# The last product of a fused attention and two-MLP kernel, from a plain tiled product to Strassen's seven products in [column, token] layout

## The chip, the cores and the metric

The kernel runs on one core of one Trainium2 chip. A core has five engines with queues of their own: TensorE (PE, matrix products; its weight loads are listed as PEld), VectorE (DVE), ScalarE (ACT), GpSimd (POOL) and SyncE (SP, which here only issues transfers). Sixteen DMA engines carry the transfers that SP and ACT issue. The metric is the device time of one execution in microseconds.

## The reference

Attention within chunks of 64 tokens (8 batches, 8 heads, 576 tokens, 64 wide), then two MLPs on 4608 tokens of 512 columns, in float32:

```python
x = attention(q, k, v)                       # 4608 x 512
h = np.maximum(x @ moe_w_in, 0.0)            # 512 -> 2048
y = h * h @ moe_w_out                        # 2048 -> 512
g = y @ moe2_w_gate                          # 512 -> 1536
val = y @ moe2_w_val                         # 512 -> 1536
out = (g * (1 / (1 + np.exp(-g))) * val) @ moe2_w_out   # 1536 -> 512
```

The last line's product, 4608 x 1536 by 1536 x 512, is what the change is about.

## The kernel before

Every float32 operand of a large product is split into a high part, rounded to the type that TensorE takes (`fp32r`), and a low part, the difference: `split` (line 419) lets ScalarE cast the high part (line 154) and VectorE subtract for the low one (line 157). `three` (line 400) then issues three matmuls, high by high, low by high and high by low, into one PSUM bank. Weights come as 64-bit words and are decoded to float32 by ScalarE, VectorE and GpSimd (`decode1` to `decode3`) before they are split.

Tokens are worked in 9 blocks of 512; `sets` pairs them as (0), (1, 2), (3, 4), (5, 6), (7, 8). The input product of the first MLP and the gate and value product of the second (class `Products`, with `Pair` for two blocks and `Single` for one) use Strassen's scheme in Winograd's form: seven products of half-sized blocks in place of eight, with sums of weights (seven combinations per pair of weight rows, `prep_pair`) and sums of tokens (`Operands`). There the weights stand in the array and 512 tokens move. A partial sum `x` in PSUM is added to by products 1, 6, 7 and 4 one after another, and ScalarE keeps copies of it on the way (`kept`, line 469; r1, u2, u3). Of the weight combinations of the gate and value product two keys of twelve stay in SBUF, the other ten are loaded again for each set (`load_combo`, line 228), three keys ahead.

The results of the gate and value product, h, are stored in DRAM (`valued`, line 591) and read back by the last product, class `Down` (line 736). It goes block by block; for each of 12 weight rows f and each of 4 groups of 128 tokens it issues `three` with the token slice of h standing and the weight row of 512 columns moving (`use2`, line 919). Four accumulators of 128 tokens by 512 columns fill four banks. At the block's end ScalarE and VectorE copy them, alternately, and SP stores each with runs of 2 KB (`evict2`, line 923). The 12 split weight rows are prepared during the last set of the gate and value product (`prep_plain`, line 165) and stay in SBUF.

The order of instructions is a planner's, which simulates the engines, except inside `ordered(...)` blocks, where the named engines keep the order of the program. TensorE's order is the program's in the gate and value product (line 909); in the last product it is the planner's. `Work` (line 233) holds prepared steps that are called beside the products: `beside2` (line 888) takes one step at every second of the 48 quarters of the last set until eight quarters before its end, then starts the last product's loads. A tile of a pool takes a buffer when one comes free; its first writer waits for that. The pool `big` has 31 buffers of 4 KB per partition, `wp` five of 14 KB, `small` six of 2 KB; PSUM has six single banks and one double one.

Of the kernel before, what the change touches and what calls it, by code (L numbers as in the profile page):

```python
# [20 lines left out]
P = 128  # L21
# [7 lines left out]
def attention_mlp_mlp_kernel(  # L29
# [135 lines left out]
    def prep_plain(name, f, raws):  # L165

        raw = raws.take(1)
        yield
        m = one("m").rearrange("p (t c) -> p t c", t=1)
        decode1(raw, m)  # L170
        decode2(raw, m)
        decode3(raw, m)
        w = duo("w", F32R)
        parts_of(m[:, 0, :], w[:, 0, :], w[:, 1, :])
        plain[name, f] = w
        yield
# [51 lines left out]
    def load_combo(key):  # L228
        w = new_combo()
        nc.sync.dma_start(out=flat(w), in_=wdram[key])  # L230
        combos[key] = w

    class Work:

# [289 lines left out]
    def dram(name, n):  # L524
        return [[dp.tile([P, 2, BLOCK], F32, name=f"{name}{b}_{i}") for i in range(n)] for b in range(nb)]

    ydram = dram("y", kt // 2)
    g1dram, g2dram = dram("g", nf1 // 2), dram("h", nf2 // 2)

    def squared(bs, fp):  # L530

# [44 lines left out]
    def valued(bs, fp):  # L576

        g = gates.pop((bs, fp))
        left = [2] * len(bs)

        def take(i, j, ps, r):
            o = g[j][:, i, :]
            if r is None:
                nc.vector.tensor_tensor(out=o, in0=ps, in1=o, op=ALU.mult)
            else:
                c = one("c")
                add(c, ps, r)
                nc.vector.tensor_tensor(out=o, in0=c, in1=o, op=ALU.mult)
            left[j] -= 1
            if left[j] == 0:  # L590
                nc.sync.dma_start(out=g2dram[bs[j]][fp], in_=g[j])

        return take


    work = Work()
    n1, n2 = nf1 // 2, nf2 // 2

    keys1 = [("i", fp) for fp in range(n1)]
    keys2 = [(name, fp) for fp in range(n2) for name in "gv"]  # L600
# [172 lines left out]
                if i == n - 1:  # L773
                    evict(b, acc)

    down1, down2 = Down(g1dram, n1), Down(g2dram, n2)

# [108 lines left out]
    def beside2(n, m):  # L888
        def at_quarter(i):
            t = 4 * m + i - 4 * len(keys2)  # L890
            if n + 1 < len(sets):
                if t == -24:
                    for b in sets[n + 1]:
                        yraw[b] = load_y(b)
                if t == -8:
                    y_sums(n + 1)
                if t in OPS:
                    up2.ops[n + 1].make(*OPS[t])
            else:
                if t % 2 == 0 and t < -8:  # L900
                    work.step(1)
                if t == -8:
                    down2.begin()
                if t == -4:
                    down2.split(0)

        return at_quarter

    with ordered(ET.PE):
        for n in range(len(sets)):  # L910
            if n + 1 == len(sets):
                raws = Raws(w_out2, 2)
                for f in range(nf2):
                    work.add(prep_plain("p", f, raws))
            for m in range(len(keys2)):
                up2.run(n, m, beside2(n, m))
        up2.finish()

    def use2(acc, t, w, g, first, last):
        cols = slice(t * P, (t + 1) * P)  # L920
        three(acc, (g[0][:, cols], g[1][:, cols]), (w[:, 0, :], w[:, 1, :]), first, last)

    def evict2(b, acc):
        for t in range(4):
            o = one("o")
            (nc.vector.tensor_copy if t % 2 else nc.scalar.copy)(out=o, in_=acc[t])
            nc.sync.dma_start(out=out[b * BLOCK + t * P:b * BLOCK + (t + 1) * P, :], in_=o)

    down2.run("p", use2, evict2, lambda b, i: work.step(1))


# [48 lines left out]
```

## Time and profile before

| | before |
|---|---|
| median of 3 runs | 1717.14 us (1717.08 to 1720.78) |
| profiled execution | 1717.07 us, span 1715.3 us |
| mean granted TensorE clock | 0.984 |
| busy TensorE, VectorE, ScalarE, GpSimd | 96%, 51%, 45%, 8% |
| DMA | 385.05 MB, mean 224 GB/s |

The span runs from the first to the last instruction; the rest of the time lies around it. In the rows further below, times are in microseconds and a mean of one instruction in ns; L157 is line 157 of the kernel. In the windows the engines stand in the order PE, PEld, DVE, ACT, POOL, each with its busy time and its count of instructions. A matmul's record is longer than the step from one to the next, because matmuls are pipelined. "idle before" is the time for which an engine stood idle ahead of an instruction, and the names behind it are what ended that.

### The profile page before, as it was taken

To read this page: it belongs to the slowest core of one execution; us is meant where nothing else is said; L and a number is where in the kernel's file an instruction comes from. 1 tells how busy PE (TensorE), PEld (TensorE's weight loads), DVE (VectorE), ACT (ScalarE), POOL (GpSimd) and SP (SyncE) were. 2 spreads that over 40 slices of the span, in tenths; PEclk is the share of its full clock that TensorE was granted. 3 is DMA by queue.
4 is the path that set the end of the run, shared out by engine and by line. 5 is a ranking of instruction groups with operands and counts; after the bars stand their busy time and mean duration, and the time that the engine had idled before them with its cause. 6 is when DMAs were issued, how large, how long until landed. Compare 5 with 4: busy or idle time off the path is not lost.

```text
span 1715.3 us, 23439 instructions
## 1 busy us (share of the span) xinstructions
PE 1641.8 (96%) x9552; PEld 1353.1 (79%) x9552; DVE 880.9 (51%) x1094; ACT 770.4 (45%) x1090; POOL 130.0 (8%) x94
## 2 busy tenths in 40 slices
PE   3878999999999999999999999999999999999998
PEld 3756777778888888888888788787887888888887
DVE  7875464645477656652313547446556666222220
ACT  5775676768775444442212434334335444222210
POOL 3220000010122111100000000000000110000000
PEclk9889999999999999999999999999999999999999
DMA  8557687878875767773329566566668855334431
GB/s 334 208 221 241 240 291 251 290 267 292 321 257 215 289 250 289 270 288 123 111 85 378 195 256 236 207 250 221 220 229 309 308 178 208 117 119 146 123 99 49
DMA packets 88380, 385.05 MB, mean 224 GB/s; under 512 B 9552, under 2 KB 9552, under 8 KB 77392
## 3 DMA queue, kind: packets, MB, share of 16 engines
q1 hardware_dynamic: 77904, 345.80, 57.2%
q10 hardware_dynamic: 10368, 37.75, 5.8%
q8 instruction: 75, 1.23, 0.3%
q14 instruction: 33, 0.27, 0.0%
HBM read 267.91 MB, written 112.46 MB: 222 GB/s over the span
## 4 chain that ended last, share of the span: by engine, by line
PE 87%; DVE 5%; DMA 4%; ACT 2%; issue 1%; SPq 1%; POOL 0%; ACTq 0%; DVEq 0%; POOLq 0%
PE acc L404 10%; PE acc L405 10%; PE acc L403 10%; PE px L403 8%; PE px L405 8%; PE px L404 8%; PE pz L405 4%; PE py L403 4%; PE pz L404 4%; PE pz L403 4%; PE py L405 4%; PE py L404 4%; PE accs L404 4%; PE accs L403 4%; PE accs L405 4%; DMA k<-in_k_dram 4%
## 5 line engine op out<-in xcount | busy, mean ns | idle before, releaser
L157 DVE TENSOR_TENSOR lo<-graw,hi 128x1024 fp32r<-128x1024 f32 x126 | 157.0, 1249 | 222.6 <-PE acc L404 153.9
L403 PE MATMUL px<-hi,W 128*128 128x512 f32 x640 | 251.9, 394 | 5.7 <-ACT hi L154 5.5
L405 PE MATMUL px<-lo,W 128*128 128x512 f32 x640 | 250.2, 391 | 3.1 <-DVE lo L157 3.1
L404 PE MATMUL px<-hi,W 128*128 128x512 f32 x640 | 249.8, 390 | 0.0
L154 ACT CAST hi<-graw 128x1024 fp32r<-128x1024 f32 x126 | 132.2, 1050 | 231.9 <-DVE lo L157 192.6
L139 POOL TENSOR_TENSOR m<-m,raw 128x512 int32<-128x512 int32 x68 | 93.1, 1383 | 1042.0 <-DVE m L135 899.3
L471 ACT COPY u<-px 128x512 f32<-128x512 f32 x160 | 92.5, 578 | 154.6 <-PE px L405 154.6
L403 PE MATMUL acc<-hi,w 128*128 128x512 f32 x416 | 161.8, 389 | 0.0
L404 PE MATMUL acc<-hi,w 128*128 128x512 f32 x416 | 161.8, 389 | 0.0
L405 PE MATMUL acc<-lo,w 128*128 128x512 f32 x416 | 161.5, 389 | 0.0
L403 PEld LDWEIGHTS px<-hi,W 128*128 128x128 f32 x640 | 120.9, 189 | 32.7 <-ACT hi L154 6.3
L405 PEld LDWEIGHTS px<-lo,W 128*128 128x128 f32 x640 | 120.5, 188 | 29.5 <-DVE lo L157 4.2
L404 PEld LDWEIGHTS px<-hi,W 128*128 128x128 f32 x640 | 120.9, 189 | 24.9
L572 DVE TENSOR_TENSOR g<-g,sig 128x1024 f32<-128x1024 f32 x54 | 69.5, 1287 | 132.5 <-ACT sig L571 132.5
L457 DVE TENSOR_TENSOR g<-pz,u 128x512 f32<-128x512 f32 x112 | 76.9, 687 | 113.6 <-PE pz L405 73.6
L403 PE MATMUL pz<-hi,W 128*128 128x512 f32 x320 | 125.8, 393 | 5.4 <-ACT hi L154 5.4
L405 PE MATMUL pz<-lo,W 128*128 128x512 f32 x320 | 126.2, 394 | 3.3 <-DVE lo L157 3.3
L403 PE MATMUL py<-hi,W 128*128 128x512 f32 x320 | 128.1, 400 | 0.0
L405 PE MATMUL py<-lo,W 128*128 128x512 f32 x320 | 126.2, 394 | 0.3 <-DVE lo L157 0.3
L404 PE MATMUL py<-hi,W 128*128 128x512 f32 x320 | 126.3, 395 | 0.0
L404 PE MATMUL pz<-hi,W 128*128 128x512 f32 x320 | 125.5, 392 | 0.0
L404 PE MATMUL acc<-w,lo 128*128 128x512 f32 x312 | 121.4, 389 | 0.0
(103 smaller groups left out, 2878.5 us busy)
## 6 DMA issues: line engine op xcount, KB each, us to landing
W<-wv SPq DMA_DIRECT2D x30, 1792.0 KB, 8.4
g<-g ACTq DMA_DIRECT2D x72, 512.0 KB, 4.8
graw<-g SPq DMA_DIRECT2D x72, 512.0 KB, 4.4
W<-wi SPq DMA_DIRECT2D x20, 1792.0 KB, 9.2
W<-wg SPq DMA_DIRECT2D x20, 1792.0 KB, 7.9
h<-g SPq DMA_DIRECT2D x54, 512.0 KB, 7.6
graw<-h SPq DMA_DIRECT2D x54, 512.0 KB, 3.7
raw<-in_w_out_dram SPq DMA_DIRECT2D x28, 512.0 KB, 8.0
```

The lines of the kernel that those rows point to most:

```text
L139: nc.gpsimd.tensor_tensor(out=mi[:, t, :], in0=mi[:, t, :], in1=word(raw, 0, I32), op=ALU.add)
L154: nc.scalar.copy(out=hi, in_=src)
L157: nc.vector.tensor_tensor(out=lo, in0=src, in1=hi, op=ALU.subtract)
L403: nc.tensor.matmul(out=ps, lhsT=lh, rhs=rh, start=first, stop=False, skip_group_check=on)
L404: nc.tensor.matmul(out=ps, lhsT=ll, rhs=rh, start=False, stop=False, skip_group_check=on)
L405: nc.tensor.matmul(out=ps, lhsT=lh, rhs=rl, start=False, stop=last, skip_group_check=on)
L457: nc.vector.tensor_tensor(out=o, in0=ps, in1=r, op=ALU.add)
L471: nc.scalar.copy(out=r, in_=self.x)
L572: nc.vector.tensor_tensor(out=g[j], in0=g[j], in1=s, op=ALU.mult)
```

## The change

The last product now uses the seven products as well, with columns standing and tokens moving. For pairs of blocks, the contraction's 1536 rows are cut into even and odd halves of h by the index c, the 512 output columns into two halves. `prep_last` decodes a pair of weight rows, forms the seven combinations of 128x256, splits them and stores them in DRAM (`vdram`), one tensor for each product; it replaces `prep_plain` in the last set, with more steps taken per quarter. `load_last` brings all six pairs of one product's weights into one `wp` buffer, or, for products 7 and 3, into three `big` buffers. Class `Last` runs the products in the order `PAIR`, each summed over all six pairs (2 halves of 128 columns, `three` for each: 36 matmuls) in two PSUM banks before the next begins; the single block uses four products, `SINGLE`. Operands are made one product ahead (`make`), with differences written in place by VectorE. `turned_out` adds a kept copy where there is one, lets VectorE transpose 32x32 blocks into the tile z, and stores z when both output halves are in it: four transfers for each half of 128 columns, whose runs in DRAM are 64 columns, 256 bytes. h is laid out as [partition, c, pair, token], so it is stored in runs of 2 KB and read in runs of 4 KB. The last stage stands inside `ordered(ET.PE)`.

```diff
@@ -229,6 +229,67 @@
         w = new_combo()
         nc.sync.dma_start(out=flat(w), in_=wdram[key])
         combos[key] = w
+    n2 = nf2 // 2
+    vdram = [dp.tile([P, n2, 2, half], F32, name=f"v{r}") for r in range(7)]
+    last_weights = {}
+    def prep_last(fp, raws):
+        pair = raws.take(2)
+        yield
+        m = duo("m")
+        decode1(pair, m)
+        yield
+        decode2(pair, m)
+        yield
+        decode3(pair, m)
+        view = m.rearrange("p t (q e i j) -> p t i e q j", q=4, e=2, i=2)
+        def columns(t):
+            return t.rearrange("p (e q j) -> p e q j", e=2, q=4)
+        def stage(src, roles):
+            t = big.tile([P, 2, len(roles), half], F32R, tag="big", name="vt")
+            for n, part in enumerate(src):
+                high(part, columns(t[:, 0, n, :]))
+                low(part, columns(t[:, 0, n, :]), columns(t[:, 1, n, :]))
+            for n, r in enumerate(roles):
+                nc.sync.dma_start(out=vdram[r][:, fp], in_=t.bitcast(F32)[:, :, n, :])
+        a11, a12, a21, a22 = view[:, 0, 0], view[:, 1, 0], view[:, 0, 1], view[:, 1, 1]
+        stage([a11, a12], [0, 1])
+        yield
+        stage([a22], [2])
+        yield
+        s = big.tile([P, 4, half], F32, tag="big", name="s")
+        s1, s2, s3, s4 = (columns(s[:, i, :]) for i in range(4))
+        tt = nc.vector.tensor_tensor
+        tt(out=s1, in0=a21, in1=a22, op=ALU.add)
+        tt(out=s2, in0=s1, in1=a11, op=ALU.subtract)
+        tt(out=s3, in0=a11, in1=a21, op=ALU.subtract)
+        tt(out=s4, in0=a12, in1=s2, op=ALU.subtract)
+        yield
+        stage([s1, s2], [3, 4])
+        yield
+        stage([s3, s4], [5, 6])
+        yield
+    def load_last(product, apart=False):
+        r = ROLES[product]
+        if not apart:
+            v = wp.tile([P, n2, 2, half], F32R, tag="W", name="V")
+            nc.sync.dma_start(out=v.bitcast(F32), in_=vdram[r])
+            last_weights[product] = [v[:, i] for i in range(n2)]
+            return
+        last_weights[product] = []
+        for i in range(0, n2, 2):
+            v = big.tile([P, 2, 2, half], F32R, tag="big", name="V")
+            nc.sync.dma_start(out=v.bitcast(F32), in_=vdram[r][:, i:i + 2])
+            last_weights[product] += [v[:, 0], v[:, 1]]
     class Work:
@@ -524,8 +585,8 @@
     def dram(name, n):
         return [[dp.tile([P, 2, BLOCK], F32, name=f"{name}{b}_{i}") for i in range(n)] for b in range(nb)]
-    ydram = dram("y", kt // 2)
-    g1dram, g2dram = dram("g", nf1 // 2), dram("h", nf2 // 2)
+    ydram, g1dram = dram("y", kt // 2), dram("g", nf1 // 2)
+    hdram = [dp.tile([P, 2, nf2 // 2, BLOCK], F32, name=f"h{b}") for b in range(nb)]
     def squared(bs, fp):
...
-                nc.sync.dma_start(out=g2dram[bs[j]][fp], in_=g[j])
+                nc.sync.dma_start(out=hdram[bs[j]][:, :, fp, :], in_=g[j])
...
@@ -773,7 +834,143 @@
                 if i == n - 1:
                     evict(b, acc)
-    down1, down2 = Down(g1dram, n1), Down(g2dram, n2)
+    def turned_out(bs):
+        z = [[big.tile([P, BLOCK // SQ, 2, SQ], F32, tag="big", name="z") for _ in range(2)] for _ in bs]
+        left = [[2, 2] for _ in bs]
+        def take(i, j, e, ps, r):
+            if r is not None:
+                o = one("o")
+                add(o, ps, r)
+                ps = o
+            nc.vector.transpose(out=z[j][e][:, :, i, :], in_=ps.rearrange("p (b t) -> p b t", t=SQ))
+            left[j][e] -= 1
+            if left[j][e] == 0:
+                rows = out[bs[j] * BLOCK:(bs[j] + 1) * BLOCK, :]
+                rows = rows.rearrange("(b r) (q e c) -> q e r b c", r=SQ, q=4, e=2)
+                for qd in range(4):
+                    nc.sync.dma_start(
+                        out=rows[qd, e],
+                        in_=z[j][e][qd * SQ:(qd + 1) * SQ].rearrange("p b i t -> p b (i t)"),
+                    )
+        return take
+    SINGLE = (1, 5, 2, 4)
+    PAIR = (1, 5, 6, 2, 7, 4, 3)
+    class Last:
+        def __init__(self):
+            self.raw, self.ops = {}, {}
+            self.seq = [(n, p) for n, bs in enumerate(sets) for p in (PAIR if len(bs) == 2 else SINGLE)]
+        def load(self, b, c):
+            self.raw[b, c] = []
+            for i in range(0, n2, 2):
+                t = duo("h")
+                nc.sync.dma_start(out=t, in_=hdram[b][:, c, i:i + 2, :])
+                self.raw[b, c].append(t)
+        def make(self, n, p):
+            bs, raw, tt = sets[n], self.raw, nc.vector.tensor_tensor
+            ops = []
+            def less(a, b):
+                for x, y in zip(raw[a], raw[b]):
+                    tt(out=y, in0=x, in1=y, op=ALU.subtract)
+                    ops.append(split(y))
+            b0, b1 = bs[0], bs[-1]
+            if len(bs) == 1:
+                if p == 5:
+                    return
+                if p == 4:
+                    less((b0, 1), (b0, 0))
+                else:
+                    ops = [split(x) for x in raw[b0, 0 if p == 1 else 1]]
+            elif p in (1, 2, 3):
+                ops = [split(x) for x in raw[{1: (b0, 0), 2: (b0, 1), 3: (b1, 1)}[p]]]
+            else:
+                less(*{
+                    5: ((b1, 0), (b0, 0)), 6: ((b1, 1), (b0, 0)), 7: ((b1, 1), (b1, 0)), 4: ((b0, 1), (b0, 0))
+                }[p])
+            self.ops[n, p] = ops
+        def product(self, ps, n, p, op, first, last=True, on=False):
+            w, ops = last_weights[p], self.ops[n, op]
+            for i in range(n2):
+                hi, lo = ops[i // 2]
+                for e in range(2):
+                    cols = slice(e * P, (e + 1) * P)
+                    three(
+                        ps[e],
+                        (w[i][:, 0, cols], w[i][:, 1, cols]),
+                        (hi[:, i % 2, :], lo[:, i % 2, :]),
+                        first and i == 0,
+                        last and i == n2 - 1,
+                        on,
+                    )
+        def kept(self, ps, name):
+            r = [one(name), one(name)]
+            for e in range(2):
+                nc.scalar.copy(out=r[e], in_=ps[e])
+            return r
+        def two(self, name):
+            return [bank(name), bank(name)]
+        def take_all(self, i, j, ps, r):
+            for e in range(2):
+                self.take(i, j, e, ps[e], r and r[e])
+        def run(self, m):
+            n, p = self.seq[m]
+            if p == 1:
+                self.take = turned_out(sets[n])
+            if len(sets[n]) == 1:
+                if p == 1:
+                    self.y = self.two("py")
+                    self.product(self.y, n, 1, 1, True, False)
+                elif p == 5:
+                    self.y1 = self.two("py")
+                    self.product(self.y1, n, 5, 1, True, False)
+                elif p == 2:
+                    self.product(self.y, n, 2, 2, False)
+                    self.take_all(0, 0, self.y, None)
+                else:
+                    self.product(self.y1, n, 4, 4, False)
+                    self.take_all(1, 0, self.y1, None)
+            elif p == 1:
+                self.x = self.two("px")
+                self.product(self.x, n, 1, 1, True)
+                self.r1 = self.kept(self.x, "r1")
+            elif p == 5:
+                self.z = self.two("pz")
+                self.product(self.z, n, 5, 5, True)
+            elif p == 6:
+                self.product(self.x, n, 6, 6, False, on=True)
+                self.u2 = self.kept(self.x, "u2")
+            elif p == 2:
+                y = self.two("py")
+                self.product(y, n, 2, 2, True)
+                self.take_all(0, 0, y, self.r1)
+            elif p == 7:
+                self.product(self.x, n, 7, 7, False, on=True)
+                self.take_all(1, 1, self.z, self.kept(self.x, "u3"))
+            elif p == 4:
+                self.product(self.x, n, 4, 4, False, on=True)
+                self.take_all(1, 0, self.x, None)
+            else:
+                self.product(self.z, n, 3, 3, False, on=True)
+                self.take_all(0, 1, self.z, self.u2)
+    down1, down2 = Down(g1dram, n1), Last()
@@ -897,12 +1094,16 @@
                 if t in OPS:
                     up2.ops[n + 1].make(*OPS[t])
             else:
-                if t % 2 == 0 and t < -8:
-                    work.step(1)
+                work.step(2 if t % 4 == 0 else 1)
                 if t == -8:
-                    down2.begin()
+                    work.step(1000)
+                    down2.load(sets[0][0], 0)
+                    load_last(1)
+                    load_last(5)
                 if t == -4:
-                    down2.split(0)
+                    down2.make(0, 1)
+                if t == -1:
+                    down2.load(sets[0][0], 1)
         return at_quarter
@@ -910,23 +1111,33 @@
         for n in range(len(sets)):
             if n + 1 == len(sets):
                 raws = Raws(w_out2, 2)
-                for f in range(nf2):
-                    work.add(prep_plain("p", f, raws))
+                for fp in range(n2):
+                    work.add(prep_last(fp, raws))
             for m in range(len(keys2)):
                 up2.run(n, m, beside2(n, m))
         up2.finish()
-    def use2(acc, t, w, g, first, last):
-        cols = slice(t * P, (t + 1) * P)
-        three(acc, (g[0][:, cols], g[1][:, cols]), (w[:, 0, :], w[:, 1, :]), first, last)
-
-    def evict2(b, acc):
-        for t in range(4):
-            o = one("o")
-            (nc.vector.tensor_copy if t % 2 else nc.scalar.copy)(out=o, in_=acc[t])
-            nc.sync.dma_start(out=out[b * BLOCK + t * P:b * BLOCK + (t + 1) * P, :], in_=o)
-
-    down2.run("p", use2, evict2, lambda b, i: work.step(1))
+    last = down2
+    load_last(2)
+    load_last(4)
+    load_last(6)
+    with ordered(ET.PE):
+        for m, (n, p) in enumerate(last.seq):
+            if n + 1 < len(sets):
+                after = sets[n + 1]
+                if p == 1:
+                    last.load(after[0], 0)
+                elif p == (4 if n else 2):
+                    last.load(after[1], 0)
+                elif p == 3 or (n == 0 and p == 4):
+                    last.load(after[1], 1)
+                    last.load(after[0], 1)
+            if m == 1:
+                load_last(7, True)
+                load_last(3, True)
+            if m + 1 < len(last.seq):
+                last.make(*last.seq[m + 1])
+            last.run(m)
 # ---- launch: one core; inputs and outputs as the reference has them ----
```

## Rows read from the trace of the kernel before

**Rows 1.** The page's busy times (us, share of span, instructions) and its packet line.
```profile
PE 1641.8 (96%) x9552; PEld 1353.1 (79%) x9552; DVE 880.9 (51%) x1094; ACT 770.4 (45%) x1090; POOL 130.0 (8%) x94
...
DMA packets 88380, 385.05 MB, mean 224 GB/s; under 512 B 9552, under 2 KB 9552, under 8 KB 77392
```

**Rows 2.** The page's chain that ended last, shares of the span by engine.
```profile
PE 87%; DVE 5%; DMA 4%; ACT 2%; issue 1%; SPq 1%; POOL 0%; ACTq 0%; DVEq 0%; POOLq 0%
```

**Rows 3.** Windows: stretch, its length, busy us by engine, granted clock, DMA share, GB/s.
```profile
890.00:930.00 40.00, 40.00 (x178) 33.13 (x177) 9.90 (x12) 7.29 (x10) 0.00 (x0) 1.00 0.93 343
1200.00:1300.00 100.00, 100.00 (x441) 82.79 (x440) 55.86 (x71) 37.04 (x54) 0.00 (x0) 1.00 0.65 236
1311.00:1426.00 115.00, 112.93 (x498) 92.87 (x497) 77.29 (x113) 54.37 (x83) 13.06 (x10) 1.00 0.65 232
1426.00:1710.00 284.00, 284.00 (x1255) 235.16 (x1254) 76.13 (x73) 64.29 (x70) 3.00 (x2) 1.00 0.39 124
1630.00:1640.00 10.00, 10.00 (x46) 8.29 (x45) 1.57 (x3) 2.11 (x2) 0.00 (x0) 1.00 0.36 105
1675.00:1685.00 10.00, 10.00 (x46) 8.29 (x45) 1.38 (x2) 1.17 (x2) 0.00 (x0) 1.00 0.28 105
```

**Rows 4.** Timeline of TensorE in the last product: start, us, engine, line, operation.
```profile
1690.26 0.39 PE L403 MATMUL acc<-w,hi 128*128 128x512 f32 x1
...
1699.10 0.39 PE L403 MATMUL acc<-w,hi 128*128 128x512 f32 x1
```

**Rows 5.** Timeline of the last microseconds: SP's stores and the last matmul.
```profile
1710.11 2.05 SPq L927 DMA_DIRECT2D out_dram<-o  x4
...
1710.43 0.39 PE L405 MATMUL acc<-w,hi 128*128 128x512 f32 x1
```

**Rows 6.** Timeline of VectorE: five operations merged in one row.
```profile
1433.54 5.76 DVE L157 TENSOR_TENSOR lo<-graw,hi 128x1024 fp32r<-128x1024 f32 x5
```

**Rows 7.** Groups by line and shape: busy us, mean ns, idle before and releasers.
```profile
L157 DVE TENSOR_TENSOR lo<-graw,hi 128x1024 fp32r<-128x1024 f32 x126 | 157.0, 1249 | 222.6 <-PE acc L404 153.9 <-ACT hi L154 39.1 <-issue 28.6
...
L154 ACT CAST hi<-graw 128x1024 fp32r<-128x1024 f32 x126 | 132.2, 1050 | 231.9 <-DVE lo L157 192.6 <-DMA graw<-g 20.3 <-PE acc L405 15.0
...
L471 ACT COPY u<-px 128x512 f32<-128x512 f32 x160 | 92.5, 578 | 154.6 <-PE px L405 154.6
...
L457 DVE TENSOR_TENSOR g<-pz,u 128x512 f32<-128x512 f32 x112 | 76.9, 687 | 113.6 <-PE pz L405 73.6 <-ACT u L471 39.7
...
L157 DVE TENSOR_TENSOR w<-m,w 128x512 fp32r<-128x512 f32 x28 | 21.8, 779 | 2.4 <-ACT w L154 2.0
...
L350 DVE STREAM_TRANSPOSE z<-e 128x1024 f32<-128x1024 f32 x12 | 14.9, 1242 | 19.4 <-POOL e L311 19.4
...
L157 DVE TENSOR_TENSOR W<-m,W 128x256 fp32r<-128x256 f32 x20 | 8.3, 416 | 0.0
```

**Rows 8.** Waits: TensorE from 800 us on, SP's DMA queue from 1311 to 1426.
```profile
PE pz L403 <- ACT hi L154: 5.4, 4, 1.3
PE pz L405 <- DVE lo L157: 2.9, 4, 0.7
...
SPq L230 <- PE pz L405: 33.1, 7, 9.5
```

**Rows 9.** DMA issues: operation, count, KB each, median us to landing.
```profile
W<-wv SPq DMA_DIRECT2D x30, 1792.0 KB, 8.4
...
out_dram<-o SPq DMA_DIRECT2D x36, 256.0 KB, 2.3
```

**Rows 10.** Issues of two lines on SP: ns min/median/max.
```profile
L927 SPq DMA_DIRECT2D out_dram<-o x36: 332/337/1019, 1449.0 to 1711.8; - x36
...
L358 SPq DMA_DIRECT2D p<-z x48: 507/583/1013, 147.4 to 377.6; - x48
```

**Rows 11.** Timeline of TensorE where the gate and value product ends.
```profile
1420.98 0.39 PE L405 MATMUL px<-lo,W 128*128 128x512 f32 x1
...
1422.34 0.39 PE L403 MATMUL pz<-hi,W 128*128 128x512 f32 x1
```

More of the change, by code (lines that the diff above doesn't have):

```diff
@@ L590, in take @@
             if left[j] == 0:
-                nc.sync.dma_start(out=g2dram[bs[j]][fp], in_=g[j])
+                nc.sync.dma_start(out=hdram[bs[j]][:, :, fp, :], in_=g[j])
         return take
     work = Work()
-    n1, n2 = nf1 // 2, nf2 // 2
+    n1 = nf1 // 2
     keys1 = [("i", fp) for fp in range(n1)]
```

## The prediction

> **What bounds the kernel now.** I began with the busy times: TensorE works 96% of the span, VectorE 51%, ScalarE 45% [rows 1]. The chain of waits agrees: 87% of it is TensorE [rows 2]. As shares are means over stages, I then cut the span into stretches. From 1426 to 1710 us, the last product alone, TensorE is busy all 284.00 us at a granted clock of 1.00, the 2.4 GHz level; VectorE is busy for 76 us of them and the DMA engines for a share of 0.39 [rows 3]. So in the stage that the change rewrites every matmul is on the path and the rest has room. The timeline gives a matmul's price: between the first and the last of 40 matmuls that follow each other (39 steps) lie 1699.10 - 1690.26 = 8.84 us, 0.2267 us a step [rows 4]. (Its 0.39 us is the length of one in the pipeline, not the step.) With the weights standing and the tokens moving, as the new product has it, the step is the same: 441 in 100 us from 1200 to 1300 [rows 3]. At the end, the last matmul is over at 1710.82, SP has issued the last store at 1712.16, the span ends at 1715.3: a tail of 4.5 us [rows 5].
>
> **The matmuls.** Before: 9 blocks x 12 f x 4 token groups x 3 = 1296. After: the single block 4 products x 6 pairs x 2 halves x 3 = 144; a pair of blocks 7 x 36 = 252, four times 1008; together 1152. It removes 144: 144 x 0.2267 = **-32.6 us**. A product of 36 now takes 8.16 us, a pair of blocks 57.1 us. What follows is what can eat this.
>
> **VectorE beside a pair of blocks.** It now makes 12 in-place differences of 128x1024 (three for each of products 5, 6, 7, 4) and 21 low parts: 33 x 1.15 us (five low parts in a row take 5.76) = 38.0 [rows 6]; six sums with a PSUM operand at 0.69 and eight transposes of 128x512, for which I take half of the 128x1024 transpose, 0.62, up to the 0.69 of a sum [rows 7]: 9.1 to 9.7. In all 47.4 of 57.1 us: hidden, but no longer with much room; in a product that carries six such operations and two sums and two transposes it has 6.9 + 2.7 = 9.6 us of work against 8.16 and must have run ahead. ScalarE has 21 casts at 1.05 and six copies at 0.58, 25.5 us [rows 7]. Of the 31 big buffers, V7 and V3 hold 6, the raw tiles of the pair 12, the prefetch of the next 3 and more, the operands of two products up to 12, the turned results 4: more than 31, so a cast often waits until TensorE has used up a third of the product before. A third is 2.7 us, the cast and low part 2.3 [rows 7]: it comes in time as long as VectorE is not behind. I price late operands at 0.5 us a pair, 2 us in all: at each of the four set changes of the products before, where operands were also made just ahead, matmuls waited up to 1.3 us for a cast and 0.7 for a low part [rows 8]. Bounds: 0, and 2.3 us in two of seven products, 18 us.
>
> **A wait that is new.** Product 4 accumulates into the banks of product 7 right behind it, and must wait until ScalarE has copied both (u3). The first half ends 0.68 us before the second and its copy takes 0.58 [rows 7], so about 0.3 us shows; where a cast of 1.05 us is ahead on ScalarE, 1.3. Behind the waiting matmul stands all of TensorE's queue, as its order is fixed. I take 0.6, four times: **+2.4** (1.2 to 5.2).
>
> **Stores in 256-byte runs.** A block of 1 MB now leaves as 8 DMAs of 512 runs, 4096 packets, 256 for each of 16 DMA engines, where it was 4 DMAs of 128 runs of 2 KB [rows 9]. No row shows data packets that small, so the price X of one is bounded. In the stretch 1675 to 1685 only four such stores run: a share of 0.28 x 10 us x 16 engines / 512 packets = 87 ns for 2 KB [rows 3]. Below: by bytes, an eighth, 11 ns. Above: no better than the 2 KB packet, 87 ns. The nearest row is the 2 KB packet, but its 375 GB/s while busy says that it is paid mostly by bytes, so I take the middle in ratio, 30 ns. The Trainium skill, DMA: Bandwidth & Descriptors, Specifications, speaks against the change here: line rate needs at least 512 bytes, and below that the engine reads, modifies and writes. No run here shows it; as an estimate, a read and a write of 256 bytes at the rate of that row would be 22 ns, and the sum below would be some 2 us smaller. Loads: in 1630 to 1640, 0.36 x 10 x 16 us for 105 GB/s x 10 us = 256 packets of 4 KB, 225 ns each [rows 3]; the 12 loads of a pair are 96 packets an engine, 21.6 us. With 512 X for the stores of a pair the DMA engines have 21.6 + 15.4 = 37 of 57.1 us: hidden. Only from X = (57.1 - 21.6) / 512 = 69 ns would they set the pace.
>
> **The tail.** With product 3 the whole last block becomes ready at once, 1 MB where it was the last of four column groups. After the last matmul (T): sum and transpose of the first half to T + 0.7, of the second to T + 1.9; eight issues at 0.34 (128 runs) to 0.58 us (the 32-partition store of the attention) [rows 10], T + 3.5 to T + 5.5; transfers from T + 0.9 on, 8 x 32 x 30 ns = 7.7 us, and some 0.6 for what is left of the other block, which started at T - 6.2: T + 9.2; then the 2.4 us that pass now between the last issue's end and the span's end beyond the 0.7 of a 256 KB transfer [rows 5]. T + 11.6 against T + 4.5: **+7**. Bounds: X = 11, issue-bound, +2; X = 87, both blocks' stores one after the other from T - 6.2, 44.5 us, +36.
>
> **The change of stage.** The old last product was left to the planner, which put its first matmuls into the gaps of the last two-sided product: between the last px at 1420.98 and the next pz at 1422.34 stand five acc matmuls [rows 11]. Now TensorE's order is written out there, with nothing to fill such a gap: 1.36 - 0.23 = 1.1 us, with the shorter one before it **+1.5** (0 to 4).
>
> **The last set of the gate and value products.** The weights of the last product are now turned into seven combinations and stored: 42 stores of 256 KB, 11.0 MB, and V1 and V5 (1.57 MB each) and three operand tiles are loaded before the set ends, in place of the first four tiles of the old product (2.1 MB). The stretch 1311 to 1426 moves 232 GB/s x 115 us = 26.7 MB [rows 3]; now 26.7 + 11.0 + 3.1 + 1.6 - 2.1 = 40.3 MB, which at 343 GB/s, what the DMA engines gave from 890 to 930 at a share of 0.93 [rows 3], take 117.5 us: 2.5 more than the set lasts. W loads, on which TensorE depends, share the queue with them; SP already waits 33.1 us for W buffers there [rows 8], and every store queued ahead of a W load makes it later. VectorE gets 11 operations of 128x256 (0.42) for each of six pairs in place of 12 low parts of 128x512 (0.78) [rows 7]: 27.5 - 9.3 = 18 us on the 77 of this stretch [rows 3], 83% of it. I take **+3** (0: some of the preparation started before the set's begin, and may again; 12: one W load, 8.4 us to land [rows 9], late by all of that and half again). That h is stored in 2 KB runs instead of 4 KB costs nothing by bytes; no engine waits for it in that stage.
>
> **Sum.** The profiled execution took 1717.07 us, of which 1.8 lie outside the span; the median of the runs is 1717.14, the same. 1717.07 - 32.6 + 2 + 2.4 + 7 + 1.5 + 3 = 1700.4; I say **1700**.
>
> **Rivals.** (A) The forecast, 1693 to 1707: 0.55.
> (B) The 256-byte packets decide. If one costs as much as a 2 KB packet, 87 ns, the DMA engines need 44.5 + 21.6 = 66.1 us a pair, 9 more than TensorE, for the three pairs that load a successor, 27 us, and the tail is +36: 1717 - 32.6 + 27 + 36 + 6.9 = 1754, slower. The tail alone turns the sum positive from 512 X - 8.3 us = 23.7, X = 63 ns. For it: the 9552 packets under 2 KB are all under 512 B too [rows 1], 16 for each of the 597 transfers, that is their completion writes; no data packet shorter than 2 KB shows a lower price. Against it: 375 GB/s while busy, which looks like a price by bytes. 0.15.
> (C) The last gate and value set is bound by DMA: a W load or V1 comes late by more than 10 us: 1700 + 11 = 1711. For it 40.3 MB against 39.4 that fit; against it three W loads of lead and a queue that throttles itself. 0.13.
> (D) VectorE or the 31 buffers set the pace of the pairs: operands late in two products of seven, 18 us in place of 2: 1716. For it 83% load in a strict order; against it the free product 1 and the light first block. 0.11.
> (E) All covers hold, X = 11: 1717 - 32.6 + 2 = 1687. 0.06.
>
> **How the numbers follow.** About 0.3% (5 us) can be told from no change. Faster: A, E, 0.08 of C, 0.03 of D: 0.72. Same (1712 to 1722): 0.04 of C, 0.05 of D: 0.09. Slower: B, 0.01 of C, 0.03 of D: 0.19. The range 1686 to 1724 holds A, E and nearly all of C and D, 0.83; B alone lies beyond.
>
> **What would show it.** TensorE: 1152 matmuls in the last stage at 0.227 us, idle of some 0.6 us ahead of each product 4 (released by ScalarE's copy), a gap of about a microsecond before the first product. DMA share between two pairs near 0.65; near 0.9 speaks for B. From last matmul to the end 11.6 us: under 8 means X near 11 ns, over 25 means B. In the last gate and value set, TensorE idle on W is C; in the pairs, idle released by lo is D. I am wrong if the tail or the pairs carry a loss of 10 us more than this.

## The result, and the profile after

The changed kernel takes 1703.2 us (median of 3 runs, 1701.5 to 1705.7) against 1717.14: a ratio of 0.9914, interval 0.9886 to 0.9941. With five rounds on another chip it was 0.9901 (0.9884 to 0.9917). The profiled execution took 1701.53 us, 15.5 less than the one before (forecast: 16.7 less, in the text rounded to 17).

The page of the changed kernel, busy times and packets (they answer to [rows 1]), and the chain (to [rows 2]):

```profile
PE 1612.9 (95%) x9408; PEld 1324.9 (78%) x9408; DVE 1023.0 (60%) x1268; ACT 817.4 (48%) x1165; POOL 130.9 (8%) x94
...
DMA packets 140367, 407.10 MB, mean 240 GB/s; under 512 B 47840, under 2 KB 57056, under 8 KB 128736
...
PE 82%; DMA 6%; DVE 6%; ACT 2%; issue 2%; SPq 1%; POOL 1%; DVEq 0%; ACTq 0%; POOLq 0%
```

144 matmuls are gone (9552 to 9408), and TensorE is busy for 28.9 us less. VectorE is busy for 142 us more. The chain leaves TensorE more often than before: 82% in place of 87%. The windows say where (columns as in [rows 3]):

```profile
1311.00:1373.00 62.00, 56.24 (x238) 44.84 (x238) 52.38 (x93) 34.75 (x68) 9.81 (x6) 0.97 0.96 358
1373.00:1426.00 53.00, 51.77 (x227) 42.02 (x226) 42.92 (x68) 25.50 (x45) 5.68 (x4) 1.00 0.99 380
1426.00:1456.00 30.00, 30.00 (x134) 24.86 (x133) 17.19 (x17) 9.39 (x9) 0.00 (x0) 1.00 1.02 414
1456.00:1480.00 24.00, 20.39 (x87) 15.58 (x86) 17.24 (x17) 7.49 (x9) 0.00 (x0) 1.00 0.51 162
1480.00:1690.00 210.00, 210.00 (x922) 172.30 (x921) 163.84 (x167) 87.90 (x97) 0.00 (x0) 1.00 0.40 118
```

From 1480 us to the end the pairs of blocks run with TensorE busy throughout and VectorE at 78%. The losses stand earlier. The engine is idle for 5.8 us between 1311 and 1373 and for 1.2 between 1373 and 1426, both in the last gate and value set, and for 3.6 between 1456 and 1480, at the first pair. The DMA share is 0.96 to 1.02 from 1311 to 1456, with up to 414 GB/s. The timeline of TensorE names the larger losses. These are rows with idle time ahead, in brackets the idle time and what ended it, and the last matmul:

```profile
1315.53 0.64 PE L464 MATMUL pz<-hi,W 128*128 128x512 f32 x1 [4.32 <-ACT hi L154]
...
1317.09 0.79 PE L466 MATMUL pz<-lo,W 128*128 128x512 f32 x1 [0.49 <-DVE lo L157]
...
1346.54 0.50 PE L464 MATMUL px<-hi,W 128*128 128x512 f32 x1 [0.56 <-ACT r L532]
...
1420.64 0.50 PE L464 MATMUL px<-hi,W 128*128 128x512 f32 x1 [0.68 <-ACT u L532]
...
1466.08 0.50 PE L464 MATMUL pz<-hi,V 128*128 128x512 f32 x1 [1.62 <-ACT hi L154]
...
1474.15 0.50 PE L466 MATMUL pz<-lo,V 128*128 128x512 f32 x1 [1.08 <-DVE lo L157]
...
1690.55 0.39 PE L466 MATMUL pz<-lo,V 128*128 128x512 f32 x1
```

For the account I took, from the last set's begin on, the time between the starts of neighbouring matmuls beyond the step of 0.2267 us [rows 4]; it includes what shows as a slower step and not as idle. Before it is 2.6 us in all, after 16.0:

| place | before | after | forecast of the difference |
|---|---|---|---|
| begin of the last gate and value set | 2.6 | 6.6 | } 3, put down to DMA |
| waits on ScalarE's copies within that set | 0 | 2.6 | } |
| end of the gate and value set (1420.64) | 0 | 0.9 | 1.5, at another place |
| product 5 and 6 of the first pair (1464 to 1478) | - | 4.7 | 2, spread over the pairs |
| ahead of the four products 4 | - | 1.1 | 2.4 |
| from the last matmul's end to the span's end | 4.5 | 8.8 | +7 |

The expectations below put the tail at 8.9, from rounded times. The differences sum to 4.0 + 2.6 + 0.9 + 4.7 + 1.1 + 4.3 = 17.6 us against the 32.6 of the matmuls; the stretch up to the set's begin was 1.2 us shorter in this execution (px L466 at 1310.83 where it was 1312.03), and 0.7 us stay unassigned: -32.6 + 17.6 - 1.2 + 0.7 = -15.5.

What stood ahead of the cast at the set's begin is on ScalarE's timeline (vt are the new combinations, split; hi<-x is the cast that TensorE waits for). After that the copy r, which ends the wait at 1346.54, stood behind a decode that waited for its raw weights:

```profile
1311.78 0.71 ACT L154 CAST vt<-m 128x256 fp32r<-128x256 f32 x2 [0.90 <-DVE m L144]
...
1313.82 0.71 ACT L154 CAST vt<-s 128x256 fp32r<-128x256 f32 x2
1314.43 1.04 ACT L154 CAST hi<-x 128x1024 fp32r<-128x1024 f32 x1
...
1345.35 0.67 ACT L130 ACTIVATE raw<-raw 128x512 int32<-128x512 uint32 x1 [2.82 <-DMA raw<-in_w_out_dram]
1345.92 0.56 ACT L532 COPY r<-px 128x512 f32<-128x512 f32 x1
```

### The profile page after: what moved, and what is told of

Same layout as the page of the kernel before. It is cut to its first block, busy times and chain, and to the rows that moved or that the text cites. A ratio compares the mean times of both kernels' runs of the same rounds, so it can differ in the third digit from the quotient of the medians.

```text
span 1699.8 us, 23601 instructions
## 1 busy us (share of the span) xinstructions
PE 1612.9 (95%) x9408; PEld 1324.9 (78%) x9408; DVE 1023.0 (60%) x1268; ACT 817.4 (48%) x1165; POOL 130.9 (8%) x94
## 4 chain that ended last, share of the span: by engine, by line
PE 82%; DMA 6%; DVE 6%; ACT 2%; issue 2%; SPq 1%; POOL 1%; DVEq 0%; ACTq 0%; POOLq 0%
PE px L464 10%; PE px L466 10%; PE px L465 9%; PE acc L464 6%; PE acc L466 6%; PE acc L465 6%; PE py L464 5%; PE pz L466 5%; PE py L465 5%; PE py L466 5%; PE pz L465 5%; PE pz L464 5%; DMA k<-in_k_dram 4%; PE accs L464 2%; PE accs L466 2%; PE accs L465 2%
## 5 line engine op out<-in xcount | busy, mean ns | idle before, releaser
L466 PE MATMUL px<-lo,W 128*128 128x512 f32 x640 | 250.4, 391 | 3.6 <-DVE lo L157 3.6
L466 PE MATMUL acc<-lo,w 128*128 128x512 f32 x416 | 161.5, 389 | 0.0
L466 PEld LDWEIGHTS px<-lo,W 128*128 128x128 f32 x640 | 120.7, 189 | 29.8 <-DVE lo L157 4.4
L633 DVE TENSOR_TENSOR g<-g,sig 128x1024 f32<-128x1024 f32 x54 | 65.9, 1220 | 125.7 <-ACT sig L632 125.6
L157 DVE TENSOR_TENSOR lo<-graw,hi 128x1024 fp32r<-128x1024 f32 x72 | 91.4, 1269 | 82.7 <-PE acc L465 42.8
L154 ACT CAST hi<-h 128x1024 fp32r<-128x1024 f32 x93 | 95.4, 1053 | 92.0 <-DVE h L885 21.9
L466 PE MATMUL pz<-lo,W 128*128 128x512 f32 x320 | 126.5, 395 | 3.1 <-DVE lo L157 3.1
L466 PE MATMUL py<-lo,W 128*128 128x512 f32 x320 | 125.9, 393 | 0.0
L157 DVE TENSOR_TENSOR lo<-h,hi 128x1024 fp32r<-128x1024 f32 x93 | 110.1, 1211 | 12.2 <-ACT hi L154 6.8
```

The lines of the kernel that those rows point to most:

```text
L154: nc.scalar.copy(out=hi, in_=src)
L157: nc.vector.tensor_tensor(out=lo, in0=src, in1=hi, op=ALU.subtract)
L466: nc.tensor.matmul(out=ps, lhsT=lh, rhs=rl, start=False, stop=last, skip_group_check=on)
L633: nc.vector.tensor_tensor(out=g[j], in0=g[j], in1=s, op=ALU.mult)
```

## The experiments

All build on the changed kernel. The first 400 us vary by some microseconds between executions (the last matmul ahead of the last set's begin came at 1310.8 and 1307.4 us in two of the changed kernel, and up to 1315.2 in kernels that are the same up to there), so places are compared by the traces and totals with that in mind.

**The removed matmuls put back.**

```diff
                 self.product(y, n, 2, 2, True)
+                self.product(y, n, 2, 2, True)
                 self.take_all(0, 0, y, self.r1)
```

> In each of the four pairs of blocks product 2 is issued twice into the same banks, the second time from a cleared start, so that exactly the 144 matmuls that the change removed come back and nothing else changes. Theory A (a matmul of the last stage is worth its step, all else lies beside it): 144 x 0.2267 = +32.6 us on the changed kernel's 1703, so 1736, above the kernel before; the idle of TensorE elsewhere stays. Rival (the pairs are paced by VectorE or DMA, and matmuls are partly hidden): clearly less than +32.6, under +25.

Measured: 1733.2 us, 1.0083 of the kernel before (1.0054 to 1.0111). From the set's begin to the last matmul's start 412.45 us in place of 379.72: +32.7 for 144 matmuls, 0.227 each. The other losses stood at the same places and came to the same sum, though not each to the same size: the set's begin lost 8.0 in place of 6.6, the rest of the set 1.5 in place of 2.6. The medians differ by 30.0 us. So a matmul of this stage is worth its whole step, and the saving of 32.6 us is shown.

**Stores in long runs.**

```diff
-                rows = rows.rearrange("(b r) (q e c) -> q e r b c", r=SQ, q=4, e=2)
+                rows = rows.rearrange("(q e r s) c -> q e r (s c)", q=4, e=2, r=SQ)
...
-                        in_=z[j][e][qd * SQ:(qd + 1) * SQ].rearrange("p b i t -> p b (i t)"),
+                        in_=z[j][e][qd * SQ:(qd + 1) * SQ].rearrange("p b i t -> p (b i t)"),
```

> Only the place of the results in the output changes: each turned half tile of 32 partitions goes out as 32 runs of 4 KB in place of 512 runs of 256 bytes, same bytes, same eight transfers a block. Theory A (the small runs cost little: about 20 ns a packet by the changed kernel's trace, hidden in the pairs, and the tail is bound by eight issues of 0.55 us): the tail of 8.9 us after the last matmul shortens by less than 2 us, the total by 0 to 2. Rival B (256-byte packets decide the tail): the tail falls to about 5 us, the total by 4 or more. If the issue gets cheaper with 32 runs than with 512, that part is the issue's.

This kernel leaves the results at other places of the output than the reference, so it serves to measure and no more. Measured: 1702.3 us (0.9910, 0.9877 to 0.9943), the same as the changed kernel. The tail is 7.8 us (1689.52 to 1697.3) in place of 8.8. The issues of the changed kernel, then of this one (ns min/median/max):

```profile
L853 SPq DMA_DIRECT2D out_dram<-z x72: 315/516/2549, 1456.4 to 1696.2; - x72
```

```profile
L853 SPq DMA_DIRECT2D out_dram<-z x72: 314/414/1224, 1455.0 to 1694.1; - x72
```

The run length costs 1.0 us in the tail, and eight issues at 0.10 us less make up most of it. Beyond that the 256-byte packets cost nothing that shows in the time. Their price can be read where only stores run, in the changed kernel:

```profile
1682.50:1690.00 7.50, 7.50 (x35) 6.22 (x34) 1.03 (x2) 0.00 (x0) 0.00 (x0) 1.00 0.67 140
```

0.67 x 7.5 us x 16 engines = 80 us for 4096 packets: 19.6 ns, where bytes alone would be 11 [rows 3] and a 2 KB packet costs 87.

**The preparation begun later, in the same set.**

```diff
-                work.step(2 if t % 4 == 0 else 1)
+                if t >= -44:
+                    work.step(2 if t % 3 == 0 else 1)
```

> The preparation of the last weights starts four quarters after the last gate and value set has begun, at a slightly higher rate, and still ends before the same point. Theory 1 (the 6.6 us that TensorE loses at the set's begin, 2.6 before the change, come from casts and copies of the preparation that stand ahead of the operands' casts on ScalarE and VectorE): the loss falls back to 2.6, total about -4. Theory 2 (they come from DMA being full): no change there, and more W or V waits later.

Measured: 1703.7 us (0.9919, 0.9895 to 0.9943), no gain. The idle at the set's begin grew from 4.32 to 6.50 us. ScalarE's timeline there:

```profile
1313.24 0.66 ACT L129 ACTIVATE m<-raw 128x512 f32<-128x512 f32 x1 [3.48 <-DMA raw<-in_w_out_dram]
...
1314.35 1.03 ACT L154 CAST hi<-x 128x1024 fp32r<-128x1024 f32 x1
```

The edit did not take the preparation away from this place: the planner now put a decode ahead of the operands' cast (L154), where casts of the preparation had been, and the decode stood at the head of ScalarE's queue for 3.48 us until its raw weights landed. The cast that TensorE needs waited behind it. So the order on ScalarE is at work, as theory 1 says, but this edit could not show it by removing it; and the transfer of the raw weights has its part here.

**V7 and V3 asked for later, and ScalarE in the program's order.** Two edits against the loss at 1464 to 1478:

```diff
-            if m == 1:
+            if m == 4:
                 load_last(7, True)
+            if m == 6:
                 load_last(3, True)
```

> V7 and V3 (six tiles of 512 KB) are asked for three and five products later. In the changed kernel the DMA engines are full (share 1.02) from 1425 to 1456 us, and product 5 of the first pair then loses 4.7 us on late operands. Theory 1 (full DMA engines make the operands' loads late): the 4.7 us go, total about -4. Theory 2 (on ScalarE the copies r1, which wait for product 1, stand ahead of the operands' casts; the DMA is not the cause): the 4.7 us stay.

```diff
-    with ordered(ET.PE):
+    with ordered(ET.PE, ET.Activation):
         for m, (n, p) in enumerate(last.seq):
```

> In the last stage ScalarE keeps the program's order too, so the casts of the next product's operands stand ahead of the copies of the product before. Theory 2 of the experiment with late V (the copies r1 ahead of the casts cost the 4.7 us at product 5 of the first pair): they go, total about -4. Theory 1 (loads late because DMA is full): they stay. Risk on the other side: copies behind casts make product 4's wait for u3 longer, 0.3 to up to 3 us a pair, since three casts of 1.05 us may stand ahead.

Measured: 1700.9 us (0.9901, 0.9876 to 0.9927) and 1699.4 us (0.9878, 0.9859 to 0.9898). In both traces TensorE waits for no cast or low part in the last stage: the 4.7 us are gone either way, and from the set's begin to the last matmul's start it takes 375.0 and 374.8 us in place of 379.7. (The totals alone, beside 1703.2 and 1701.8 for the changed kernel, are too close to tell.) By its expectation each result supports its own theory, so ScalarE's timelines have to decide. The changed kernel, then V later, then ScalarE in order (r is the copy that waits for product 1 to end):

```profile
1450.89 1.06 ACT L154 CAST hi<-h 128x1024 fp32r<-128x1024 f32 x1 [0.94 <-PE py L466]
1463.81 1.26 ACT L922 COPY r<-px 128x512 f32<-128x512 f32 x2 [11.86 <-PE px L466]
1464.98 1.99 ACT L154 CAST hi<-h 128x1024 fp32r<-128x1024 f32 x2
```

```profile
1457.92 1.05 ACT L154 CAST hi<-h 128x1024 fp32r<-128x1024 f32 x1 [6.17 <-DVE h L885]
1462.04 1.05 ACT L154 CAST hi<-h 128x1024 fp32r<-128x1024 f32 x1 [3.08 <-DVE h L885]
1463.78 1.05 ACT L154 CAST hi<-h 128x1024 fp32r<-128x1024 f32 x1 [0.68 <-DVE h L885]
1468.29 1.27 ACT L922 COPY r<-px 128x512 f32<-128x512 f32 x2 [3.46 <-PE px L466]
```

```profile
1462.26 2.19 ACT L154 CAST hi<-h 128x1024 fp32r<-128x1024 f32 x2 [6.30 <-DVE h L885]
1465.80 1.05 ACT L154 CAST hi<-h 128x1024 fp32r<-128x1024 f32 x1 [1.35 <-PE px L466]
1467.82 1.27 ACT L922 COPY r<-px 128x512 f32<-128x512 f32 x2 [0.97 <-PE px L466]
```

In the changed kernel ScalarE stood 11.86 us in front of the copies, with the casts of product 5's operands behind them, though VectorE had made the differences for the first two from 1456.97 on (the third came only at 1467.20, behind the first low part, which itself waited for a cast):

```profile
1456.97 2.32 DVE L885 TENSOR_TENSOR h<-h 128x1024 f32<-128x1024 f32 x2
```

In both experiments the three casts come before the copies. And with ScalarE in order, where V7 and V3 are asked for as in the changed kernel, the DMA engines are as full as ever in the stretch before, so full DMA engines by themselves are not the cause (with V later the share and the rate are the same):

```profile
1426.00:1456.00 30.00, 30.00 (x134) 24.84 (x133) 19.25 (x21) 9.39 (x9) 0.00 (x0) 1.00 1.02 415
```

The order on ScalarE is the cause: the edit that changes that order alone removes the loss. Asking for V7 and V3 later also led the planner to put the casts first; that run moved the operands' loads ahead too, and what did it there is not separated. The risk named for the strict order (a longer wait ahead of product 4) did not come: 0.27 us as before.

**The preparation over two sets.**

```diff
+                if n + 2 == len(sets) and -40 <= t < -8:
+                    work.step(1)
             else:
-                work.step(2 if t % 4 == 0 else 1)
+                if -40 <= t:
+                    work.step(1)
...
-            if n + 1 == len(sets):
+            if n + 2 == len(sets):
                 raws = Raws(w_out2, 2)
```

> The same preparation, begun a set earlier and spread over the two last gate and value sets (32 steps in the one, the rest from the eighth quarter of the other), none around the change of sets. Theory 1 (ordering on ScalarE and VectorE at the set's begin): the 6.6 us there fall to 2.6, and the waits of about 0.6 us on ScalarE's copies within the set (2.6 us in all) thin out: -5. Theory 2 (DMA is full in the last set and that costs): the DMA share there falls from 0.96 to about 0.85, and the gain is larger than 5, as V1 and the first loads of the pairs come sooner too. No gain at all would say that the preparation's place does not matter.

Measured: 1694.4 us (0.9857, 0.9842 to 0.9872). From the set's begin to the span's end 378.15 us in place of 388.92, 10.8 less. TensorE's waits from 1290 us to the end, first of the changed kernel, then of this one (total, times, longest):

```profile
PE pz L464 <- ACT hi L154: 5.9, 2, 4.3
PE pz L466 <- DVE lo L157: 2.1, 3, 1.1
PE px L464 <- ACT r L532: 1.1, 2, 0.6
PE px L464 <- ACT u L532: 1.1, 2, 0.7
PE px L466 <- DVE lo L157: 0.4, 1, 0.4
```

```profile
PE pz L464 <- ACT hi L154: 1.3, 1, 1.3
PE pz L466 <- DVE lo L157: 0.7, 1, 0.7
```

What is left are the waits that the kernel before had at this place [rows 8]; half-speed matmuls behind them (last section) bring the set's begin to 4.2 us, against the 2.6 expected. Nothing of the preparation stands ahead of the cast there any more:

```profile
1315.79 1.06 ACT L632 ACTIVATE sig<-g 128x1024 f32<-128x1024 f32 x1
1316.76 1.03 ACT L154 CAST hi<-x 128x1024 fp32r<-128x1024 f32 x1
```

Nearly all of the waits on copies (2.6 us to 0.3), the 0.9 us at the end of the set and the 4.7 us at the first pair are gone. The DMA share fell from 0.96 to 0.90 in 1311 to 1373 and from 0.99 to 0.79 behind it. The expectation's theory 1 holds for what was lost at the set's begin and in it; for the rest ScalarE's order changed here as well (the casts again come before the copies), so the share of the DMA in the gain is not separated.

The move has a price in the set before. No matmul of the changed kernel starts late there; with this edit TensorE waits for a weight load that lands late (until 1280.56), while the DMA share is 0.99 to 1.05 from 1260 to 1282 us:

```profile
PE px L464 <- DMA W<-wg: 1.8, 1, 1.8
```

With the half-speed matmuls behind that wait and a shorter delay at 1224 us the set before loses 4.0 us, so about 6.8 of the 10.8 us remain. The medians differ by 8.8 us, the profiled executions by 5.5.

**The tail.**

```diff
-                    nc.sync.dma_start(
+                    queue = nc.scalar if bs[j] == nb - 1 and qd % 2 else nc.sync
+                    queue.dma_start(
...
-            for i in range(n2):
+            at_end = (n, p) == self.seq[-1]
+            order = [(i, e) for i in range(n2) for e in range(2)]
+            if at_end:
+                order = [(i, e) for e in range(2) for i in range(n2)]
+            for i, e in order:
```

> Two edits at the end: the last product of all finishes its first 128 columns before it begins the second 128, and half of the last block's stores are issued by ScalarE's queue. Theory (the tail is issue and VectorE work after the last matmul): the first half's sum, transpose and stores move beside 4 us of matmuls, and four issues of 0.55 remain in two queues: the tail falls from 8.9 to 5 to 6 us, total -3 to -4. Rival (the tail is the landing of 256-byte packets): it falls by at most 1 to 2 us.

Measured: 1699.6 us (0.9882, 0.9863 to 0.9900). The tail is 6.6 us in place of 8.8, 2.2 less: below the 3 to 4 expected and above the rival's 1 to 2. The end of the changed kernel, then of this one:

```profile
1690.29 1.37 DVE L518 TENSOR_TENSOR o<-pz,u 128x512 f32<-128x512 f32 x2 [6.76 <-PE pz L466]
1691.58 1.29 DVE L847 STREAM_TRANSPOSE z<-o 128x512 f32<-128x512 f32 x2
...
1692.31 4.44 SPq L853 DMA_DIRECT2D out_dram<-z  x8
```

```profile
1692.60 0.69 DVE L518 TENSOR_TENSOR o<-pz,u 128x512 f32<-128x512 f32 x1 [2.64 <-PE pz L466]
1693.32 0.71 DVE L847 STREAM_TRANSPOSE z<-o 128x512 f32<-128x512 f32 x1
```

SP's issues fill 1692.31 to 1696.75 in the changed kernel: issue and VectorE work make up 5.8 of the 8.8 us. With half of it moved ahead, one sum, one transpose, the last two issues on each queue and the landing remain. The two edits were not tried apart.

**Both gains in one kernel, beside the changed kernel again.**

> The preparation over two sets and both edits of the tail in one kernel. They act in places that don't meet, so their gains should add: about -10.8 us from the gate and value set's begin to the first pair of blocks, -2.3 us in the tail, against the changed kernel in the same rounds; about 1690. Rival (the gains overlap, for example because the pairs are now paced by VectorE): less than -10.

> The changed kernel as it is, timed on the same chip as the combination, with five rounds for a narrower interval: about 0.991 of the kernel before, 15 us less. TensorE's idle places (6.6 us at the set's begin, 4.7 at product 5 of the first pair, about 0.26 ahead of each product 4) should come back at the same places, as the order of instructions is fixed; the first 400 us may vary by some us.

The first run has the edits of the two experiments above, the second no edit. Measured: 1691.9 us (0.9836, 0.9821 to 0.9851) and 1701.8 us (0.9901, 0.9884 to 0.9917). From the set's begin to the span's end 376.0 us against 388.7 in the changed kernel's repetition, 12.7 less: from there on the gains add (10.8 + 2.2 = 13.0). The medians differ by 9.9 only, which by itself would fall on the rival's side. In the profiled executions, which differ by 5.1, the combination came to the set's begin 7.6 us later: 5.8 of that in the first 400 us, which vary, and 1.7 as the price of the moved preparation in the set before. The losses of the repeated kernel stood at the same places: 4.41 us of idle at the set's begin, 1.62 at product 5, and steps longer by 0.16 and 0.11 at each product 4. The combination is the fastest of all, 1.6% below the kernel before.

## Why the prediction was right, and where its terms were off

- *What bounds the stage, and the 32.6 us:* right, and shown by putting the matmuls back.
- *VectorE beside the pairs:* right. From 1500 to 1650 us VectorE is busy for 123.6 of 150 us, 82%, forecast 47.4 of 57.1, 83%, and TensorE waits for no operand. The 31 buffers cost nothing that shows in the pairs.

```profile
1500.00:1650.00 150.00, 150.00 (x659) 123.01 (x658) 123.56 (x126) 65.55 (x72) 0.00 (x0) 1.00 0.51 153
```

- *Late operands, 2 us:* mis-sized and misplaced. They cost 4.7 us, all at the first pair and nothing in the other three. The step looked at the amount of work and at buffers; what decided was the order on ScalarE, where a copy that must wait for TensorE stood ahead of casts that could have gone.
- *The wait for u3, 2.4 us:* 1.1. No cast stood ahead of the copies; the bare 0.3 us a pair was the right end of the bounds.
- *Packets and tail, 7 us:* 4.3. X is 19.6 ns and not 30, and the DMA share in the pairs 0.51 where 0.65 was forecast. On the rule of the Trainium skill, DMA: Bandwidth & Descriptors, Specifications (below 512 bytes the engine reads, modifies and writes), the estimate was 22 ns; the trace agrees with its size, though it does not show the mechanism. With 20 ns the other block's stores had left the queue before the last ones came, and the tail became a matter of issue. The eight issues took 0.55 us each, near the dear end of the 0.34 to 0.58 that the step allowed; so its lower bound of +2 for cheap packets, worked out with 0.34, was too low as well.
- *Change of stage, 1.5 us:* 0.9, but not by the step's mechanism; that the sizes are near each other is luck. The step said that nothing would fill the gap between the last px and the next pz. There the planner put 26 matmuls of the single block's first product, without a pause, although both stages stand inside `ordered`:

```profile
1421.90 0.39 PE L466 MATMUL px<-lo,W 128*128 128x512 f32 x1
1422.13 0.39 PE L464 MATMUL py<-hi,V 128*128 128x512 f32 x1
```

  The 0.9 us stand ahead of the last set's product 4 (1420.64), which waits for the copy u3. In the kernel before 22 matmuls of the last product stood at that place, from 1414.86 to 1419.62.
- *The last gate and value set, 3 us:* 6.6, from a cause that the step did not name. It priced a DMA queue that is full, and DMA was full (0.96 to 0.99). But no matmul waited for W or V. The 343 GB/s taken as the ceiling were not one: 414 GB/s passed. What cost was again ScalarE's queue, with decodes and casts of the preparation ahead of the operands' cast and of the copies. Of the 4.0 us at the set's begin about 1 us is longer steps, mostly at half speed, and not waits. Where a decode at the head waits for raw weights, the DMA has its part, and how large it is stays open.
- *Rivals:* B is out by the packet's price and the long-run stores, D by three of four pairs without a wait on operands. C's mechanism, a late W load, did not occur in the changed kernel; its place did cost, by another way. It did occur, at 1.8 us, when the preparation was moved a set ahead.

The sum comes so near in part by luck, through errors that cancel: 3.6 too little for the set and 2.7 for operands, against 2.7 too much for the tail, 1.3 for u3 and 0.6 for the change of stage.

## What to carry to other kernels

When work is added beside a bound engine, add up each helper engine's time, but then look at the order of its queue: a copy or a decode that must wait at the head stops every cast behind it, though the engine is half idle. Full DMA engines made no matmul of the changed kernel wait for a weight load; the added preparation cost through the instruction queues. Moved a set ahead it did make one load 1.8 us late, so moved work has to be priced where it goes as well as where it leaves. A saving of whole matmuls on the path was kept in full here, and what is worth tuning afterwards are the joints: the begin of the stage, the first pair, the tail.

## What the runs showed of the hardware that was not expected

A pause of TensorE can be followed by half-speed matmuls. After the 4.32 us of idle that end at 1315.53 the granted clock was 0.51 from 1317.0 to 1319.2, the 1.2 GHz level. Where no idle lies between, the steps there are 0.43 us, about 0.2 more than at the full clock:

```profile
1317.00:1319.20 2.20, 2.11 (x5) 1.73 (x6) 0.70 (x3) 0.00 (x0) 0.00 (x0) 0.51 0.90 303
```

```profile
1317.68 0.63 PE L464 MATMUL pz<-hi,W 128*128 128x512 f32 x1
1318.11 0.63 PE L465 MATMUL pz<-hi,W 128*128 128x512 f32 x1
1318.53 0.63 PE L466 MATMUL pz<-lo,W 128*128 128x512 f32 x1
1318.96 0.48 PE L464 MATMUL py<-hi,W 128*128 128x512 f32 x1
```

In the combination the same happened after pauses of only 1.34 and 0.73 us, with six steps of 0.43 in a row. In the kernel before, pauses of 1.34 and 0.72 us left the steps at 0.23 from the second matmul on: the same pauses cost about 1.5 us more in one execution than in the other.

The DMA engines moved 414 GB/s over 30 us (1426 to 1456), mostly loads with runs of 4 KB and more with two stores of 512 KB among them, well above the 343 at a share of 0.93 that the kernel before showed.
